# Chunked delta rule and two feed-forward layers: two row products as one run, Silu as the gate, and new positions

## The chip, the cores and the metric

The kernel runs on one core of one Trainium2 chip. The metric is device time in microseconds (us) of one execution, the median of the runs. The engines are TensorE (PE, with its weight loads PEld), VectorE (DVE), ScalarE (ACT), GpSimd (POOL) and SyncE (SP), which here issues the DMA requests. An SPq or PEq in a row is the engine's sequencer.

## What is computed

The inputs are q, k and v (4 batches, 8 heads, 768 positions, 48 features) and beta. Everything is float32.

```python
k_n = k / (norm(k) + 1e-06)
for t in range(S):                      # per batch and head, state is 48 x 48
    y[t] = q[t] @ state
    state = state + beta[t] * outer(k_n[t], v[t] - k_n[t] @ state)
x = y as (3072 tokens, 384)
h = x @ w_in;   x = (h * sigmoid(1.702 * h)) @ w_out      # first layer, 384 -> 2048 -> 384
h = max(x @ w_in2, 0);   out = (h * h) @ w_out2           # second layer, same sizes
```

## The kernel before

**Chunks.** The 768 positions are cut into 12 chunks of 64. Within a chunk the recurrence is a triangular system. For chunk n, `run_a` multiplies keys by keys and queries by keys (for chunk 0 `run_k` and `run_q` do this apart), `solve_in` transposes the result, `solve_norm` finds the key norms, `solve_prep` scales the rows and sets the diagonal of U (L659 to L665), and `solve_loop` inverts the triangles step by step, on POOL for most chunks. For chunks 0 and 1 (`blocks`) it works on 16 x 16 blocks (`solve_blocks`, 15 steps), which `merge` joins with two groups of matmuls. `finish` transposes U to Td (L751). Then come `scale_v` (v times the norms), `run_x` (what the state already holds for these keys), `run_w` (the first 32 rows of the solution), `run_r` (the block that links the two halves, negated back into Td at L858 and L860), `run_v` (the other 32 rows, from Td and both kinds of rows), `run_y` (the chunk's output) and `run_s` (the new state). A float32 matmul of these groups is two TensorE instructions in the trace.

**Tokens.** `run_y` leaves one chunk's 256 tokens in xf_sb; part of them is moved across partitions by six small DMAs, from Td's space (L910). Two chunks make a block of 512 tokens. The first layer takes the blocks in units: `step` is one unit (128 of the 2048 hidden rows): 9 matmuls into a bank h, the gate, and `layer2` adds 9 matmuls into three banks z. Products are exact to float32 by splitting x, the weights and the gated values into a high and a low part (three matmuls for each). The second layer runs behind the first, when no chunk is left. The first 16 units are half as wide (256 columns): 8 for chunk 0's tokens alone, then 8 for chunk 1's.

**The gate of the first layer** (L1029 to L1035): ScalarE writes g = tanh(0.851 h) from h to SBUF; VectorE writes (g + 1) h back into h (L349); ScalarE copies h rounded to ghi; VectorE writes glo = h - ghi. The factor 0.5 is applied when z is taken out.

**Weights** arrive in float32 through three buffers raw, and each is split by ScalarE (a Prelu and two copies), VectorE and VectorE or POOL (`split_w`).

**Order.** All work is put into a list by a planner (`Program`), which knows estimated costs, and sends each operation to its engine's queue in the order in which the planned engines come free; an operation with two possible queues takes the earlier one. Each engine then runs its queue in order. `TUNE` holds numbers for it: `scan`, `gscan`, `solve` and `gsolve` are positions, in units, at which a chunk's groups join the list; `conv` is how many weights are split behind each unit; `holds` makes a group of loads wait for a named result; `gate` adds such a dependence in the plan. `pad` names TensorE entries by their number and puts so many zero matmuls (512 columns, L306) ahead of each; `auto` adds zero matmuls where the plan shows a gap: its first number times the gap, less the second, up to the planned time that is its third. `fills` and `warm` place further zero matmuls, `warm` behind steps of chunk 0's solve (`keep_warm`, L669), where a matmul of one column that reads U comes ahead of them.

The first chain is chunk 0: its keys, its solve on VectorE, merge, w, r, v and `first_y`, which makes x for the first unit without the DMAs.

Of the kernel before, what the change touches and what calls it, by code (L numbers as in the profile page):

```python
# [48 lines left out]
    tiny=(0, 40),  # L49
# [16 lines left out]
class Program:  # L66
# [8 lines left out]
    def __init__(self, queues):  # L75
        self.queues = queues
        self.ops = []
        self.writer, self.readers = {}, {}
        self.free = {q: 0.0 for q in queues}
        self.dma_free = 0.0  # L80
        self.urgent = False
        self.columns = {}
        self.gate, self.idle = (), set()
        self.filler, self.n_pe, self.z_out = None, 0, []
        self.run = self.run_end = self.burst_end = 0.0
# [37 lines left out]
    def flush(self):  # L123
# [22 lines left out]
        while todo:  # L146
# [80 lines left out]
def kernel(  # L227
# [80 lines left out]
    z_open = [0]  # L308
# [341 lines left out]
    def solve_prep(n):  # L650
        s2, U = sm["s2"], U_sb[n % 2]
        gu = gu_sb[n % 2].rearrange("p (i j) -> p i j", i=32)
        K = gu_keys(n)
        if n in TUNE["blocks"]:
# [4 lines left out]
        for e in range(2):  # L659
            R, W = ["dup", "s2", ("U", n % 2)], [("U", n % 2)]  # L660
            o, x, d = U.rearrange("p c i -> p (c i)")[:, e::34], s2[:, e::2], dup_sb[:, e:e + 1]
            if n == 0:
                pg.add("pool", 0.27, lambda en, o=o, x=x, d=d: en.tensor_scalar(out=o, in0=x, scalar1=d, scalar2=None, op0=ALU.mult), R, W)
            else:
                ts(32, R, W, out=o, in0=x, scalar1=d, op0=ALU.mult)  # L665
# [14 lines left out]
    def solve_blocks(n, queue):  # L680

        gu, U = gu_sb[n % 2].rearrange("p (i j) -> p i j", i=32), U_sb[n % 2]
        for j in range(15):
# [27 lines left out]
            pg.add(queue, cost, fn, gu_keys(n) + [("U", n % 2)], [("U", n % 2)] + ((gu_keys(1) if n == 0 else ["tmp1"]) if queue == "dve" else []) + (["first"] if n == 0 and j == 14 else []))  # L711
            if n == 0:
                keep_warm(U[:, 7, j:j + 1], len(pg.ops) - 1, TUNE["warm"][j])
# [96 lines left out]
    def run_w(n):  # L810
        Td = Td_sb[n % 2]
        both, todo = groups(1), []
        for p in range(8):
            for g, ps, A, sl in both:
                for h in range(2):
                    r = 64 * h
                    o = r if g else r + 32
                    todo.append((ps[o:o + 32, p, :], Td[r:r + 32, 8 * g + p, :], w_sb[r:r + 32, 8 * g + p, :], True, True))
        mms((1.05, 1.75), todo, [("Td", n % 2)] + [("Td", n % 2, h) for h in range(2)] + [("W", g, 0, h) for g in range(2) for h in range(2)],
            [A for _, _, A, _ in both], 0.45)  # L820
        return evict_w(n, 0, both)
# [20 lines left out]
    def run_r(n):  # L842

        G, Td = G_sb[n % 2], Td_sb[n % 2]
        ps, A = bank()
        todo = []
        for a in range(NP):
            for h in range(2):
                r = 64 * h
                todo.append((ps[r:r + 32, 32 * a:32 * a + 32], G[r + 32:r + 64, a, 32:64], Td[r + 32:r + 64, a, :], True, True))  # L850
        mms((1.05, 1.75), todo, G_keys(n) + [("Td", n % 2)] + [("Td", n % 2, h) for h in range(2)], [A], 0.2)
        for h in range(2):
            r = 64 * h
            out, in_ = Td[r:r + 32], ps[r:r + 32].rearrange("p (a i) -> p a i", a=NP)

            def fn(e, out=out, in_=in_):
                if e is nc.scalar:
                    e.activation(out=out, in_=in_, func=AF.Copy, scale=-1.0)  # L858
                else:
                    e.tensor_scalar(out=out, in0=in_, scalar1=-1.0, scalar2=None, op0=ALU.mult)  # L860

            pg.add(("act", "dve"), (c_act(512, 32), c_dve(512, False, 32)), fn, [A], [("Td", n % 2, h)])

# [12 lines left out]
    def ws_keys(g):  # L876
        return [("W", g, k, h) for k in range(2) for h in range(2)]

    def run_y(n):
# [17 lines left out]
        for g, ps, A in both:  # L897
# [76 lines left out]
    def layer2(ph, j, f, c0, n, hi, lo, K):  # L974
# [385 lines left out]
```

## Time and profile before

| | us |
|---|---|
| median of 3 runs (lowest, highest) | 976.78 (976.5, 977.99) |
| the profiled execution | 979.03 |
| its span, first to last instruction | 977.2 |
| TensorE busy | 946.9 |
| VectorE busy | 522.7 |
| ScalarE busy | 459.3 |
| POOL busy | 326.1 |

The profile is one execution. An engine's busy time is the time that its instructions cover. The granted clock is the share of full speed (2.4 GHz) that TensorE had in a stretch; 0.50 is 1.2 GHz. In brackets behind an instruction stands how long its engine waited for it and which engine, tile and line released it.

### The profile page before, as it was taken

Reading aid. Unit: us, or ns where it says so; the run is one execution under the profiler, and the core shown is the slowest. Engines: PE = TensorE matmul, PEld = TensorE weight load, DVE = VectorE, ACT = ScalarE, POOL = GpSimd, SP = SyncE. Lnnn points to the kernel's source line nnn. Section 1 sums busy time; section 2 is a strip of 40 time slices with the busy share of each in tenths; the row PEclk is TensorE's granted clock in tenths of the full one; section 3 lists DMA queues with packets and bytes.
Section 4 is the critical chain, followed back from the end, with each engine's and each line's share of the span. In section 5 each row is a group of like instructions: output and inputs, shape, how many; then the busy total and the mean of one; then the engine's idle time right before and its main releaser. Section 6 shows DMA issues by size and latency. Waiting matters only on the chain.

```text
span 977.2 us, 25992 instructions
## 1 busy us (share of the span) xinstructions
PE 946.9 (97%) x11067; PEld 768.5 (79%) x11067; DVE 522.7 (53%) x1038; ACT 459.3 (47%) x934; POOL 326.1 (33%) x702
## 2 busy tenths in 40 slices
PE   7888999999999999999999999999999999999998
PEld 4567877778788878877887888888888888888886
DVE  7767975837566483656536676643433433433332
ACT  4367785444453544445346575642332422422322
POOL 3148885885857658585501000000000000000000
PEclk9679999999999999999999999999999999999999
DMA  5466561413313132221024354220010100000000
GB/s 187 161 196 210 140 203 49 132 29 102 117 65 99 50 110 68 63 79 39 17 78 155 97 159 130 67 65 1 13 52 1 52 14 1 33 0 1 33 1 33
DMA packets 34635, 75.84 MB, mean 78 GB/s; under 512 B 6326, under 2 KB 7382, under 8 KB 34518
## 3 DMA queue, kind: packets, MB, share of 16 engines
q1 hardware_dynamic: 34518, 74.17, 24.4%
q8 instruction: 87, 1.43, 0.6%
q14 instruction: 30, 0.25, 0.1%
HBM read 63.64 MB, written 9.44 MB: 75 GB/s over the span
## 4 chain that ended last, share of the span: by engine, by line
PE 77%; POOL 10%; DVE 6%; issue 3%; ACT 2%; DMA 2%; SPq 0%; POOLq 0%; ACTq 0%; DVEq 0%
PE h L369 35%; PE z L369 34%; PE a L369 7%; POOL tmpp L737 5%; POOL U L741 4%; DMA xf_sb<-Td 1%; DVE glo L342 1%; PE z L306 1%; DVE h L349 1%; DVE Td L751 1%; DVE w_sb L342 1%; ACT w_sb L331 0%; POOL wo_lo L342 0%; POOL p L543 0%; DMA k_sb<-in_kt 0%
## 5 line engine op out<-in xcount | busy, mean ns | idle before, releaser
L326 ACT ACTIVATE g_sb<-h 128x512 f32<-128x512 f32 (+1 forms) x200 | 116.0, 580 | 289.2 <-PE h L369 288.1
L369 PE MATMUL z<-ghi,wo_hi 128*128 128x512 f32 (+1 forms) x600 | 231.5, 386 | 0.0
L369 PE MATMUL z<-glo,wo_hi 128*128 128x512 f32 (+1 forms) x600 | 230.0, 383 | 0.3 <-DVE glo L342 0.3
L369 PE MATMUL z<-ghi,wo_lo 128*128 128x512 f32 (+1 forms) x600 | 229.4, 382 | 0.0
L342 DVE TENSOR_TENSOR glo<-h,ghi 128x512 fp32r<-128x512 f32 (+1 forms) x200 | 133.3, 667 | 83.4 <-ACT ghi L326 81.6
L326 ACT ACTIVATE ghi<-h 128x512 fp32r<-128x512 f32 (+1 forms) x200 | 116.0, 580 | 116.8 <-DVE h L349 58.4
L737 POOL TENSOR_TENSOR tmpp<-U,gu 128x126 f32<-128x126 f32 (+22 forms) x310 | 137.8, 445 | 84.6 <-DVE U L346 61.8
L342 DVE TENSOR_TENSOR h<-g_sb,h 128x512 f32<-128x512 f32 x96 | 66.8, 696 | 173.5 <-ACT g_sb L326 173.5
L741 POOL TENSOR_TENSOR U<-U,tmpp 128x126 f32<-128x126 f32 (+22 forms) x310 | 129.5, 418 | 24.3
L369 PEld LDWEIGHTS z<-ghi,wo_hi 128*128 128x128 f32 x600 | 113.5, 189 | 23.4
L369 PEld LDWEIGHTS z<-glo,wo_hi 128*128 128x128 f32 x600 | 113.5, 189 | 22.9 <-DVE glo L342 0.8
L369 PEld LDWEIGHTS z<-ghi,wo_lo 128*128 128x128 f32 x600 | 113.7, 190 | 22.2
L369 PE MATMUL h<-x_hi,wi_hi 128*128 128x512 f32 (+1 forms) x312 | 125.7, 403 | 4.0 <-DVE glo L342 3.0
L349 DVE SCALAR_TENSOR_TENSOR h<-g_sb,h 128x512 f32<-128x512 f32 (+1 forms) x104 | 67.6, 651 | 115.0 <-ACT g_sb L326 109.7
L369 PE MATMUL h<-x_lo,wi_hi 128*128 128x512 f32 (+1 forms) x312 | 118.3, 379 | 0.0
L369 PE MATMUL h<-x_hi,wi_lo 128*128 128x512 f32 (+1 forms) x312 | 117.7, 377 | 0.0
L369 PE MATMUL h<-x_hi,vi_hi 128*128 128x512 f32 x288 | 112.0, 389 | 0.0
L369 PE MATMUL h<-x_hi,vi_lo 128*128 128x512 f32 x288 | 112.0, 389 | 0.0
L369 PEld LDWEIGHTS h<-x_hi,wi_hi 128*128 128x128 f32 x312 | 59.7, 191 | 20.0 <-DVE glo L342 5.9
L369 PEld LDWEIGHTS h<-x_hi,wi_lo 128*128 128x128 f32 x312 | 59.8, 192 | 10.8
L369 PEld LDWEIGHTS h<-x_lo,wi_hi 128*128 128x128 f32 x312 | 59.9, 192 | 8.2
L369 PEld LDWEIGHTS h<-x_hi,vi_lo 128*128 128x128 f32 x288 | 54.0, 188 | 11.3
(153 smaller groups left out, 1133.4 us busy)
## 6 DMA issues: line engine op xcount, KB each, us to landing
raw<-in_w_in SPq DMA_DIRECT2D x32, 384.0 KB, 3.4
raw<-in_w_out SPq DMA_DIRECT2D x32, 384.0 KB, 3.7
kq<-in_kf SPq DMA_DIRECT2D x44, 256.0 KB, 3.6
kT_sb<-in_kq SPq DMA_DIRECT2D x11, 512.0 KB, 4.7
q<-in_kq SPq DMA_DIRECT2D x11, 512.0 KB, 3.8
k_sb<-in_kt SPq DMA_DIRECT2D x12, 384.0 KB, 3.8
v_sb<-in_vt SPq DMA_DIRECT2D x12, 384.0 KB, 4.7
xf_sb<-zd SPq DMA_DIRECT2D x18, 256.0 KB, 2.8
```

Of the source, the lines that this page charges most:

```text
L306: e.matmul(out=z_ps[KX - 1][:, 0:w], lhsT=z0[:, 0:128], rhs=z0[:, 0:w], start=not z_open[0], stop=not z_open[0])
L326: pg.add("act", c_act(n, kw["out"].shape[0]), lambda e: e.activation(**kw), reads, writes, early)
L342: pg.add(queue, cost, lambda e: e.tensor_tensor(out=out, in0=in0, in1=in1, op=op), reads, writes, early)
L349: pg.add("dve", c_dve(n), lambda e: e.scalar_tensor_tensor(**kw), reads, writes, early)
L369: e.matmul(out=out, lhsT=lhsT, rhs=rhs, start=start, stop=stop)
L737: e.tensor_tensor(out=t, in0=U[:, c0 + lo:c0 + hi, w:w + 1].to_broadcast(shape), in1=gu[:, :w, w:w + 1].rearrange("p i o -> p o i").to_bro ...
L741: e.tensor_tensor(out=y, in0=y, in1=t, op=ALU.add)
L751: pg.add("dve", 0.97, lambda e: e.transpose(out=Td_sb[n % 2].rearrange("p a (c e) -> p c e a", e=2), in_=U_sb[n % 2]), [("U", n % 2)], [(" ...
```

## The change

- `run_r` is gone as a function: its matmuls stand in `run_w`, each behind one of w's, in a bank of their own. Td's link block is copied behind w's rows.
- The gate is Silu(1.702 h) from h to g; ghi and glo are made from g, not from h; z is multiplied by 1/1.702. VectorE's product is gone.
- In chunk 0 the diagonal of U is set ahead of the block product, one half on POOL and one on VectorE, as separate keys; the matmul of `keep_warm` reads another column; `scale_v(0)` can run on VectorE alone.
- The load of a later chunk's queries is planned behind y's six DMAs (`behind_y`); the first queries are loaded and multiplied behind chunk 1's keys (`q_first`), and the loads behind the first keys wait for a later group (`holds`).
- Chunk 1's solve runs on POOL, chunk 2's norms on VectorE; the low parts of the second layer's weights are made on POOL alone; scaling v may go to either engine for chunks 1 to 4.
- Positions, conversions, pads and the planner's fillers have new numbers. Between z's last matmul and its copy no filler is put in.

```diff
-    warm=(0, 1, 0, 2, 0, 1, 1, 0, 1, 0, 1, 0, 0, 0, 1, 0),
-    burst=(2, 7, 120),
-    spread=1.85,
+    warm=(1, 0, 0, 1, 0, 0, 0, 0, 1, 0, 0, 3, 2, 1, 0, 1),
+    burst=(3, 2, 220),
+    spread=1.65,
...
-    slack=0.1,
+    slack=0.2,
-    q_first=1,
+    q_first=0,
-    lead=0,
-    holds=(1, 1, 1),
+    lead=80,
+    holds=(2, 1, 1),
-    conv=(3, 1, 1, 4, 0, 1, 2, 0, 1, 0, 0, 0, 0, 3, 3, 1, 1, 4, 4, 1, 2, 1, 3, 0, 0, 4, 1, 1, 7, 0, 6, 6),
-    lo_both=99,
-    v_pool=2,
+    conv=(4, 1, 0, 5, 1, 3, 1, 3, 0, 0, 0, 1, 0, 3, 0, 0, 1, 3, 4, 2, 2, 4, 1, 1, 1, 4, 1, 1, 4, 0, 3, 7),
+    lo_both=32,
+    v_pool=5,
-    solve1='dve',
-    pad={27: 2, 147: 3, 36: 4, 33: 6, 217: 1, 48: 2, 28: 3, 20: 1, 41: 1, 12: 3},
-    auto=(3.0, 1.3, 290),
-    fills=(2, 0, 0, 0),
-    norm_pool=(1, 2),
+    solve1='pool',
+    pad={217: 1, 12: 1, 41: 3, 90: 1, 11: 1, 263: 4, 35: 6, 229: 4, 50: 1, 150: 3, 154: 3, 29: 2, 226: 3, 27: 2, 259: 2, 284: 1, 31: 5, 306: 3, 309: 1, 44: 4, 143: 2, 273: 4, 180: 3, 264: 2, 34: 1, 32: 3},
+    auto=(6.0, 1.5, 620),
+    fills=(5, 0, 3, 0),
+    norm_pool=(),
-    scan={1: (-4.5, -4.5, -3.0, -2.5, -1.0, 1.0), 2: (11.5, 11.5, 11.5, 11.5, 12.5, 14.5), 3: (14.5, 19.0, 19.5, 19.5, 21.5, 22.0)},
-    gscan=(0.0, 2.0, 2.0, 3.5, 3.5, 7.5),
-    gsolve=(-9.0, -8.0, -2.5, -1.5),
-    solve={2: (-8.0, -7.0, -5.5, -2.5), 3: (3.0, 8.0, 12.0, 12.5), 4: (14.5, 19.0, 21.0, 21.5), 5: (21.5, 24.1, 30.2, 31.5)},
+    scan={1: (-1.5, -1.5, -1.0, 1.0, 1.0, 2.5), 2: (9.5, 9.5, 9.5, 9.5, 9.5, 13.5), 3: (17.0, 20.0, 20.0, 21.0, 21.0, 25.0)},
+    gscan=(1.0, 1.5, 1.5, 3.0, 4.0, 8.0),
+    gsolve=(-11.5, -10.5, -2.5, 0.5),
+    solve={2: (-10.5, -9.5, -7.5, -2.0), 3: (1.5, 6.0, 9.0, 11.5), 4: (11.0, 18.5, 20.5, 22.0), 5: (23.0, 25.1, 29.7, 31.0)},
...
-                if pad:
+                if pad and self.z_open[0] >= 0:
...
+        def diagonal(e):
+            R, W = ["dup", "s2", ("U", n % 2)], [("U", n % 2)] if n else [("U", 0, e)]
+            o, x, d = U.rearrange("p c i -> p (c i)")[:, e::34], s2[:, e::2], dup_sb[:, e:e + 1]
+            if n == 0 and e == 0:
+                pg.add("pool", 0.27, lambda en: en.tensor_scalar(out=o, in0=x, scalar1=d, scalar2=None, op0=ALU.mult), R, W)
+            else:
+                ts(32, R, W, out=o, in0=x, scalar1=d, op0=ALU.mult)
+
+        if n == 0:
+            for e in range(2):
+                diagonal(e)
...
-                keep_warm(U[:, 7, j:j + 1], len(pg.ops) - 1, TUNE["warm"][j])
+                keep_warm(U[:, 7, w - 1:w], len(pg.ops) - 1, TUNE["warm"][j])
...
-           ("dve", "pool") if n < TUNE["v_pool"] else "dve")
+           ("dve", "pool") if 0 < n < TUNE["v_pool"] else "dve")
...
     def run_w(n):
-        Td = Td_sb[n % 2]
+        G, Td = G_sb[n % 2], Td_sb[n % 2]
         both, todo = groups(1), []
+        ps_r, A_r = bank()
...
-                    r = 64 * h
+                    a, r = 8 * g + p, 64 * h
                     o = r if g else r + 32
-                    todo.append((ps[o:o + 32, p, :], Td[r:r + 32, 8 * g + p, :], w_sb[r:r + 32, 8 * g + p, :], True, True))
+                    todo.append((ps[o:o + 32, p, :], Td[r:r + 32, a, :], w_sb[r:r + 32, a, :], True, True))
+                    todo.append((ps_r[r:r + 32, 32 * a:32 * a + 32], G[r + 32:r + 64, a, 32:64], Td[r + 32:r + 64, a, :], True, True))
...
+    def behind_y(load, *args):
+
+        old = pg.gate
+        pg.gate = [y_dma[0]]
+        load(*args)
+        pg.gate = old
...
-                act(TT, [("z", e)], [key], out=zs, in_=z_ps[e], scale=0.5 if ph == 1 else 1.0)
+                act(TT, [("z", e)], [key], out=zs, in_=z_ps[e], scale=1.0 / GATE if ph == 1 else 1.0)
...
         if ph == 1:
-            act(n, [("h", p)], kg, out=g, in_=ps, func=AF.Tanh, scale=GATE / 2)
-            stt(n, [("h", p)] + kg, [("h", p)], out=ps, in0=g, scalar=1.0, in1=ps, op0=ALU.add, op1=ALU.mult)
+            act(n, [("h", p)], kg, out=g, in_=ps, func=AF.Silu, scale=GATE)
+            act(n, kg, khi, out=hi, in_=g)
+            tt(n, kg + khi, klo, lo, g, hi, ALU.subtract)
...
-            put(2, lambda: run_r(m))
...
-                put(4, *[lambda g=g: load_kq(m + 2, g) for g in range(4)], lambda: load_q(m + 2))
+                put(4, *[lambda g=g: load_kq(m + 2, g) for g in range(4)], lambda: behind_y(load_q, m + 2))
```

## Rows read from the trace of the kernel before

**Rows 1.** The page, busy us (share of the span) and instructions.
```profile
PE 946.9 (97%) x11067; PEld 768.5 (79%) x11067; DVE 522.7 (53%) x1038; ACT 459.3 (47%) x934; POOL 326.1 (33%) x702
```
**Rows 2.** Windows by stage; the first line names the columns.
```profile
core 0: us, PE busy (x) PEld busy (x) DVE busy (x) ACT busy (x) POOL busy (x), PEclk, DMA share, GB/s
...
24.80:41.80 17.00, 13.07 (x309) 8.99 (x311) 12.55 (x57) 5.63 (x13) 2.68 (x3) 0.50 0.62 204
...
58.90:69.10 10.20, 8.30 (x214) 7.69 (x215) 5.33 (x13) 8.05 (x19) 2.98 (x10) 0.50 0.44 120
69.10:100.00 30.90, 25.44 (x623) 22.21 (x622) 24.11 (x43) 23.74 (x62) 25.68 (x45) 0.94 0.70 214
100.00:185.00 85.00, 81.52 (x1473) 66.02 (x1474) 63.90 (x133) 58.30 (x133) 66.32 (x131) 0.98 0.46 140
185.00:260.00 75.00, 73.88 (x1273) 58.88 (x1272) 43.52 (x89) 34.29 (x71) 55.81 (x130) 1.00 0.21 62
...
920.00:977.20 57.20, 53.07 (x234) 43.36 (x232) 17.93 (x26) 16.77 (x28) 0.00 (x0) 1.00 0.04 14
```
**Rows 3.** Waits of TensorE: us in total, times, longest.
```profile
PE a L369 <- issue: 6.5, 5, 1.8
...
PE h L369 <- DVE glo L342: 3.0, 7, 0.7
```
**Rows 4.** Timeline of chunk 0's solve: start us, us, what [idle before].
```profile
9.84 1.06 POOL L663 TENSOR_SCALAR U<-sm_s,dup_sb 128x16 f32<-128x16 f32 x2 [2.65 <-issue]
...
10.94 0.68 DVE L697 SCALAR_TENSOR_TENSOR U<-gu,U 128x15 f32<-128x15 f32 x4 [0.56 <-POOL U L663]
...
15.31 0.30 DVE L702 TENSOR_TENSOR U<-U,gu 128x35 f32<-128x35 f32 x2 [0.61 <-PE z L672]
...
16.14 1.55 POOL L342 TENSOR_TENSOR w_sb<-v_sb,nt 128x768 f32<-128x768 f32 x1 [3.74 <-DMA v_sb<-in_vt]
...
16.27 1.57 DVE L702 TENSOR_TENSOR U<-U,gu 128x30 f32<-128x30 f32 x2
```
**Rows 5.** Timeline of TensorE: w of chunk 2, w and r later.
```profile
152.78 0.88 PE L369 MATMUL a<-w_sb,Td 32*32 32x48 f32 x64 [1.43 <-DVE Td L751]
...
358.56 0.39 PE L369 MATMUL z<-glo,wo_hi 128*128 128x512 f32 x1
358.79 0.39 PE L369 MATMUL z<-ghi,wo_lo 128*128 128x512 f32 x1
359.11 0.80 PE L369 MATMUL a<-w_sb,Td 32*32 32x48 f32 x56
...
359.80 1.14 PE L369 MATMUL a<-Td,G 32*32 32x32 f32 x61
...
361.21 0.40 PE L369 MATMUL h<-x_lo,wi_hi 128*128 128x512 f32 x1
```
**Rows 6.** Timelines of TensorE, SP and ScalarE: chunk 1's r, v, y, run_a.
```profile
70.03 1.20 PE L369 MATMUL a<-Td,G 32*32 32x32 f32 x64
...
73.14 0.88 PE L369 MATMUL a<-w_sb,Td 64*32 64x48 f32 x62 [0.45 <-DVE Td L860]
...
79.14 0.33 SPq L313 DMA_DIRECT2D q<-in_kq  x1
...
80.36 3.84 SPq L313 DMA_DIRECT2D xf_sb<-Td  x6
...
86.86 0.42 ACT L326 ACTIVATE x_hi<-xf_sb 128x256 fp32r<-128x256 f32 x1 [2.96 <-DMA xf_sb<-Td]
...
87.88 0.93 PE L369 MATMUL a<-kq 64*32 64x96 f32 x56 [2.95 <-ACT p L331]
```
**Rows 7.** Windows of the fillers (L306) alone: us, PE busy, PEld busy, clock.
```profile
185.00:260.00 75.00, 0.39 (x1) 0.10 (x1) 1.00 0.21 62
```
**Rows 8.** Groups by form: count, busy us, mean ns, idle before.
```profile
L349 DVE SCALAR_TENSOR_TENSOR h<-g_sb,h 128x512 f32<-128x512 f32 x88 | 61.0, 693 | 114.0 <-ACT g_sb L326 108.8 <-ACT xf_sb L326 4.8
...
L346 DVE TENSOR_SCALAR U<-sm_s,dup_sb 128x16 f32<-128x16 f32 x22 | 5.4, 283 | 0.0
...
L326 ACT ACT_TABLE_LOAD x2 | 2.6, 1283 | 0.8 <-PEq L1351 0.8
```

More of the change, by code (lines that the diff above doesn't have):

```diff
@@ L83, in __init__ @@
         self.gate, self.idle = (), set()
-        self.filler, self.n_pe, self.z_out = None, 0, []
+        self.filler, self.n_pe, self.z_out, self.z_open = None, 0, [], [0]
         self.run = self.run_end = self.burst_end = 0.0
@@ L658, in solve_prep @@
             tt(1024, ["s2"] + K, K, gu, gu, s2.rearrange("p (i o) -> p i o", o=1).to_broadcast([128, 32, 32]), ALU.mult)
[L659 to L665, printed above, removed]
+        if n:
+            for e in range(2):
+                diagonal(e)
     def keep_warm(gate, key, parts):
@@ L710, in solve_blocks @@
             cost = 2 * c_pool(2 * m * w) - 0.04 if queue == "pool" else 4 * (0.06 + 0.00104 * m * w) + 0.05
-            pg.add(queue, cost, fn, gu_keys(n) + [("U", n % 2)], [("U", n % 2)] + ((gu_keys(1) if n == 0 else ["tmp1"]) if queue == "dve" else []) + (["first"] if n == 0 and j == 14 else []))
+            pg.add(queue, cost, fn, gu_keys(n) + [("U", n % 2)] + ([("U", 0, e) for e in range(2)] if n == 0 else []), [("U", n % 2)] + ((gu_keys(1) if n == 0 else ["tmp1"]) if queue == "dve" else []) + (["first"] if n == 0 and j == 14 else []))
             if n == 0:
-                keep_warm(U[:, 7, j:j + 1], len(pg.ops) - 1, TUNE["warm"][j])
+                keep_warm(U[:, 7, w - 1:w], len(pg.ops) - 1, TUNE["warm"][j])
     def solve_loop(n, queue, cuts):
@@ L815, in run_w, with fn @@
                 for h in range(2):
-                    r = 64 * h
+                    a, r = 8 * g + p, 64 * h
                     o = r if g else r + 32
-                    todo.append((ps[o:o + 32, p, :], Td[r:r + 32, 8 * g + p, :], w_sb[r:r + 32, 8 * g + p, :], True, True))
-        mms((1.05, 1.75), todo, [("Td", n % 2)] + [("Td", n % 2, h) for h in range(2)] + [("W", g, 0, h) for g in range(2) for h in range(2)],
-            [A for _, _, A, _ in both], 0.45)
-        return evict_w(n, 0, both)
+                    todo.append((ps[o:o + 32, p, :], Td[r:r + 32, a, :], w_sb[r:r + 32, a, :], True, True))
+                    todo.append((ps_r[r:r + 32, 32 * a:32 * a + 32], G[r + 32:r + 64, a, 32:64], Td[r + 32:r + 64, a, :], True, True))
+        mms((1.5, 2.5), todo, G_keys(n) + [("Td", n % 2)] + [("Td", n % 2, h) for h in range(2)] + [("W", g, 0, h) for g in range(2) for h in range(2)],
+            [A for _, _, A, _ in both] + [A_r], 0.45)
+        more = evict_w(n, 0, both)
+        for h in range(2):
+            r = 64 * h
+            out, in_ = Td[r:r + 32], ps_r[r:r + 32].rearrange("p (a i) -> p a i", a=NP)
+            def fn(e, out=out, in_=in_):
+                if e is nc.scalar:
+                    e.activation(out=out, in_=in_, func=AF.Copy, scale=-1.0)
+                else:
+                    e.tensor_scalar(out=out, in0=in_, scalar1=-1.0, scalar2=None, op0=ALU.mult)
+            pg.add(("act", "dve"), (c_act(512, 32), c_dve(512, False, 32)), fn, [A_r], [("Td", n % 2, h)])
+        return more
     def evict_w(n, k, both):
@@ L840, in evict_w @@
         return more
[L842 to L862, printed above, removed]
     def run_v(n):
@@ L1033, in step @@
             tt(n, [("h", p)] + kg, [("h", p)], ps, g, ps, ALU.mult)
-        act(n, [("h", p)], khi, out=hi, in_=ps)
-        tt(n, [("h", p)] + khi, klo, lo, ps, hi, ALU.subtract)
+            act(n, [("h", p)], khi, out=hi, in_=ps)
+            tt(n, [("h", p)] + khi, klo, lo, ps, hi, ALU.subtract)
         prev.append((ph, j, f, c0, n, hi, lo, khi + klo))
@@ L1130 @@
         solve_norm(1)
-        act(32, ["nu"], ["warmed"], out=g_sb[:, 0:32], in_=z32[:, 0:32], func=AF.Tanh)
+        act(32, ["nu"], ["warmed"], out=g_sb[:, 0:32], in_=z32[:, 0:32], func=AF.Silu)
         solve_prep(1)
         more = run_w(0)
-        run_r(0)
         for x in more:
```

11 lines of the change are left out of this document (7 added, 4 removed).

## The prediction, made before the change was run

> **What bounds the kernel now.** I read the page's busy shares first: TensorE is busy 946.9 us of a span of 977.2 us [rows 1], so nearly all of the time is matmuls laid end to end, and a gain must shorten the matmul list, fill TensorE's idle 30 us, or lift its clock. The windows by stage then show where that is possible [rows 2]. From 185 us on TensorE is busy 73.88 of 75 us at full clock, so there only less TensorE work helps; at the end stand 4.1 us (57.2 less 53.07) of output that nothing here touches. The loss is early: in 24.8 to 41.8 and 58.9 to 69.1 the granted clock is 0.50 (the 1.2 GHz level); in 69.1 to 100 TensorE is idle 5.5 us; in 100 to 185 it is idle 3.5 us and the mean clock of 0.98 costs another 1.7 us. The waits of TensorE name the releasers [rows 3]: 6.5 us of "issue" (in stretches of small matmuls) and 3.0 us for glo. The timelines [rows 4 to 6] show who stands behind each.
>
> The sum is made against the profiled span of 977.2 us; that execution took 979.03 us in all, and the median of the runs, 976.78, lies 0.4 us under the span. I take off the same 0.4 us at the end.
>
> **The change part by part.**
>
> *Three waits of the first chain (9.7 to 16.3 us).* (1) Now the two diagonal products on POOL take 9.84 to 10.90 and VectorE's first solve step starts at 10.94 after 0.56 us of waiting [rows 4]. VectorE was free at 10.38; after, one of the two goes to it ahead of the block product and takes 0.28 us (L346, [rows 8]), so the solve starts at 10.66: -0.28 us. (2) The keep-warm matmul reads U's column j, which a later step overwrites; VectorE waited 0.61 us for it [rows 4]. Column w-1 is final after its step, so this wait goes: -0.61. (3) scale_v(0) ran on POOL from 16.14 for 1.55 us, and in that time two VectorE updates of 30 columns took 1.57 us, where a pair of 35 columns took 0.30 at 15.31 [rows 4]: -1.27. On VectorE it comes behind the solve, next to TensorE's first merge; if that cover is gone it costs about 1.0 us. Together **-2.1** (bounds -2.2 to 0). Late next: the queries. Their two loads now go out behind four key loads and behind a later hold, some 2 to 3 us later than at 7 us; their matmuls move behind run_a(1) and have until the solve ends, behind 17 us, so I price that at nothing; uncovered it is those 2 to 3 us, which cancels this term (the upper bound). The 80 one-column matmuls of lead run while TensorE waits for its first keys: nothing.
>
> *Chunk 1's solve from VectorE to POOL.* VectorE loses the solve's 56 small steps, between which the evictions of w and v queued in the first half-clocked stretch. POOL is free in that stretch (2.68 us busy of 17 [rows 2]). **-0.5** (bounds -2 to +1: POOL's operations slow VectorE, as under (3)).
>
> *w and r as one run.* In a full-clock chunk the last large matmul before starts at 358.79, w's 64 small ones at 359.11, r's at about 359.80, and the second large one behind starts at 361.21 [rows 5]. Large ones follow each other every 0.23 us (358.56, 358.79), so w and r cost 361.21 - 358.79 - 2 x 0.23 = 1.96 us. w takes 0.69 us for 64 (10.8 ns each), r from 359.80 to about 360.87, 1.07 us (16.7 each), the rest, 0.2, is changeover. w's go to four places of the array, r's to two, and with fewer places the pace is slower; r's places are others than w's, so in turn each gets more time. Bounds: at r's own pace the whole takes 1.07 + 0.2 (saves 0.7); without any overlap and with a dearer changeover 1.96 + 0.2 (costs 0.2). If 128 go at w's pace, the fastest in the rows, they need 1.38 us and save 0.38. I take -0.45, between that and r's own pace. Ten chunks (2 to 11), of which chunk 2 has its r apart (w alone at 152.78 [rows 5]) and saves one more changeover: **-4.8** (bounds -7.2 to +2).
> The Trainium skill, "TensorE: Matmul & The Clock Gate", section "Back-to-back issue gap", gives about 25 ns as the issue floor of a matmul of 1 to 64 columns; by it 128 would need 3.2 us and no order could gain. The trace does not agree: w's go at 10.8 ns.
>
> *The same in chunks 0 and 1.* Chunk 0: r's result is there with w's and no longer after the copies of w's last rows: **-0.7** (0 to -1.5). Chunk 1: r stands apart at 70.03, and v waits for its copies until 73.14 [rows 6]. In turn with w, which runs as soon as Td is merged, r, v and y can come some us earlier.
>
> *Queries later, y earlier.* The six requests that carry y's rows across partitions go out at 80.36, behind a 512 KB query load of 79.14; ScalarE stands at x_hi for them for 2.96 us, until 86.86, and TensorE at run_a for 2.95 us [rows 6]; then the clock falls, and the mean of 0.94 over 30.9 us costs 1.9 us [rows 2]. Put behind y, the load takes about 2.4 us out of their way (512 KB at the 214 GB/s of [rows 2]). Idle and lost clock are worth 4.8 us; but y itself is put one unit later (18 matmuls of 256 columns, 0.12 us each: 2.2 us). What waits behind the query load on SP's queue are weight loads, 2 us later, with three buffers in hand. **-3.0** (bounds -4.8 to +3).
>
> *Silu.* The product on VectorE falls away: 88 of 0.693 us and 16 shorter ones [rows 8], some 67 us of VectorE, off TensorE's path except where h is held. h is now free after the first activation, not after glo: the 3.0 us of waiting for glo [rows 3] go; in exchange g's single buffer is held until glo is read, which ends in the 4.1 us of a unit. **-2.5** (bounds -3.0 to 0).
>
> *Chunk 2.* w waits 1.43 us for the transposed Td [rows 5], then the clock falls (1.7 us lost). Its solve is asked for earlier and VectorE is lighter: **-1.5** (bounds -3.1 to +1).
>
> *Fillers.* Zero matmuls put ahead of a TensorE entry cost 0.23 us each wherever TensorE would not have waited. The old table's last entries are 147:3 and 217:1; the one filler after 185 us is the latter [rows 7]. From entry 143 on the new table has 36, 25 of them from 217 on, in place of 4: 32 x 0.23 = 7.4 us. The planner's own fillers (auto) come on top wherever it sees a gap over 0.4 us, 0.8 before. Idle there was 3.5 + 1.1 us [rows 2], and half of it is already counted as gone above. I take **+4** (bounds +1 to +7.4). The remaining positions, and the second layer's weights split on POOL alone, lie beside a gapless TensorE, which hides them: nothing; uncovered, a split on POOL is about 0.8 us (half the columns of the 1.55 us of [rows 4]), once for each unit that waits for it.
>
> Sum: -2.1 - 0.5 - 4.8 - 0.7 - 3.0 - 2.5 - 1.5 + 4.0 = -11.1; 977.2 - 11.1 - 0.4 = 965.7, say **966 us**.
>
> **The rivals.**
> *A, no overlap of w and r, or every filler in full.* For it: TensorE takes its list in order. Against: w's own four places already go faster than r's two. Without the 4.8, or with 3.4 more for fillers: 969 to 975, about 971.
> *B, the clock stays up early.* In the two stretches at 0.50 TensorE is busy 13.07 and 8.30 us, fillers included [rows 2]; at full clock at most half of it, 10.7 us, goes. For it: more zeros in the gaps (fills 2 to 8), shorter waits. Against: the issue stalls stay. I counted nothing; with 5 us: about 961, down to 956.
> *C, chunk 1 comes late.* Slower. Chunk 1's y feeds the second half of the first units; each us that its rows land after 86.8 is TensorE idle, then half-clocked, so counts about 1.6 (2.95 us idle brought 1.9 of lost clock). Its solve on POOL, y and s at later places all push it back. It decides from some 8 us later on (11.1 + 2 over 1.6); with 10 us, about 981. Against: POOL is nearly idle from 24.8 to 41.8 us [rows 2].
> *D, the tables.* Slower. A table load takes 1283 ns, and there are two in all [rows 8], though Tanh alternates with the weights' Prelu. If Silu needed another table than Prelu, some 58 loads would come before 185 us: 74 us of ScalarE, which has 34 us free between 69 and 185 [rows 2]: 40 us more than fits, about 1006. The Trainium skill, "ScalarE: Activation LUTs", section "Table sets: the hidden batching unit", says that cheap functions stand in every set; whether Prelu is one of them it does not list, and no row shows it.
> *E, no change:* gains go where TensorE is not waited for, fillers eat the rest: 975 to 978.7.
>
> **How the numbers follow.** Forecast (961 to 970) 0.43, A 0.20, B 0.19, E 0.08, C 0.07, D 0.03. About 0.2% (2 us) is what a measurement here can tell from no change. Faster is the forecast, A and B: 0.82; same 0.08; slower C and D, 0.10. The range leaves out C, D, most of E's upper half and B's last part: 956 to 976.
>
> **What would show it.** First solve step near 10.7 and no VectorE pair of 1.57 us; all behind it some 3 us earlier at chunk 0's end; w and r of a chunk together near 1.5 us; no wait of TensorE for glo; y's six requests ahead of the query load; less idle than 5.5 us before 100 us; and behind 185 us the fillers, and whether idle stands in front of them. The prediction is wrong if w and r keep 1.96 us, if the fillers stand in a gapless stretch, or if chunk 1's rows land after 90 us.

## The result, and the profile after

The changed kernel takes **989.09 us** (median; 988.31 to 989.36), the kernel before, beside it on the same chip, 976.71: a ratio of 1.0123 (95% interval 1.0105 to 1.014), 12 us slower. The prediction, 966 and faster, was wrong. The profiled execution took 988.31 us, its span is 986.6 (before 977.2). (The profiled executions of e4, e7 and e12 took far longer than the other runs of the same kernels, 1052 to 2418 us, so for those three only the other times are used.)

The windows of the changed kernel that answer to [rows 2], and one more:
```profile
24.80:41.80 17.00, 12.65 (x390) 8.44 (x394) 9.39 (x24) 10.28 (x24) 10.40 (x25) 0.63 0.76 264
58.90:69.10 10.20, 8.34 (x233) 6.99 (x234) 5.65 (x19) 2.48 (x5) 2.15 (x2) 0.83 0.25 83
69.10:100.00 30.90, 26.93 (x664) 22.63 (x650) 24.49 (x40) 24.49 (x61) 25.55 (x44) 1.00 0.63 201
100.00:185.00 85.00, 78.16 (x1464) 63.21 (x1470) 58.77 (x113) 57.90 (x130) 66.98 (x130) 1.00 0.45 141
185.00:260.00 75.00, 72.10 (x1261) 55.60 (x1264) 35.76 (x76) 32.33 (x69) 58.81 (x125) 0.98 0.20 62
260.00:520.00 260.00, 254.89 (x4081) 204.49 (x4081) 116.91 (x228) 118.20 (x234) 164.89 (x356) 0.99 0.21 67
```
The last of these windows in the kernel before:
```profile
260.00:520.00 260.00, 259.05 (x4097) 208.63 (x4096) 146.51 (x286) 120.43 (x246) 150.05 (x348) 1.00 0.23 73
```
Up to 100 us the change as a whole gained: the clock is higher in all three windows, and TensorE is idle 4.0 us (30.90 less 26.93) from 69.1 to 100, where it was 5.5 [rows 2]. Behind 100 us, and most of all behind 185 us, where the prediction saw a gapless TensorE, the gain is lost. There TensorE is idle 6.8, 2.9 and 5.1 us, together 14.85; before it was 5.55 (3.5, 1.1 and, from 260 to 520, 0.95). A count of the matmuls into h and z shows where the time goes. At 185 us the changed kernel has started 177 of those with 512 columns, the kernel before 174; at 320 us 579 and 620, and at 520 us 1272 and 1315. So nearly all of the loss arises between 185 and 320 us: 41 matmuls, at 0.23 us each 9.4 us, as much as the two profiled spans differ. VectorE is lighter (468.8 us busy in all, before 522.7), POOL heavier (375.9 for 326.1). TensorE's waits from 100 to 320 us say for whom (us in total, times, longest):
```profile
PE a L369 <- DVE Td L759: 8.2, 3, 4.5
PE z L369 <- DVE glo L342: 2.6, 2, 1.6
PE a L369 <- DVE sm_nu L566: 1.4, 1, 1.4
PE a L369 <- DVE w_sb L342: 1.0, 1, 1.0
```
The line for Td in the kernel before, same stretch:
```profile
PE a L369 <- DVE Td L751: 1.9, 2, 1.4
```
8.2 us go to three waits for Td, the solved system that comes from POOL's solve (chunks 2, 4 and 6: 1.09, 2.60 and 4.53 us). TensorE's timeline at the longest of them, and POOL's in the same stretch:
```profile
286.49 0.39 PE L369 MATMUL z<-ghi,wo_lo 128*128 128x512 f32 x1
291.41 0.28 PE L369 MATMUL a<-w_sb,Td 32*32 32x48 f32 x1 [4.53 <-DVE Td L759]
```
```profile
271.01 0.25 POOL L749 TENSOR_TENSOR U<-U,tmpp 128x31 f32<-128x31 f32 x1
271.34 1.55 POOL L745 TENSOR_TENSOR tmpp<-U,gu 128x110 f32<-128x110 f32 x1
272.97 0.41 POOL L749 TENSOR_TENSOR U<-U,tmpp 128x110 f32<-128x110 f32 x1
273.46 0.58 POOL L745 TENSOR_TENSOR tmpp<-U,gu 128x30 f32<-128x30 f32 x1
...
288.75 0.43 POOL L745 TENSOR_TENSOR tmpp<-U,gu 128x110 f32<-128x110 f32 x1
289.27 0.40 POOL L749 TENSOR_TENSOR U<-U,tmpp 128x110 f32<-128x110 f32 x1
289.74 0.22 POOL L745 TENSOR_TENSOR tmpp<-U,gu 128x16 f32<-128x16 f32 x1
290.04 0.23 POOL L749 TENSOR_TENSOR U<-U,tmpp 128x16 f32<-128x16 f32 x1
```
From 270.7 us on, chunk 7's first steps (31, 30, 58 columns) stand in turn with chunk 6's last (110, 108, 96), and chunk 6's solve, which TensorE waits for, ends at 290.3 only. Chunk 7's steps take about 10 us of that stretch, more than the 4.53 us waited. The granted clock falls to the 1.2 GHz level from 208.0 to 211.4 and from 289.9 to 296.75 us, at two of the waits for Td; the kernel before has one such stretch behind 100 us, of 3.4 us (154.4 to 157.8), and then none before the output. TensorE works in 8.7 us of the two stretches (in the second it waits until 291.41), so half clock costs some 4.4 us. Waits for Td and half clock are thus 12.6 us, for 1.9 and 1.7 before: 9.0 us more, close to what the spans differ. (The expectations below reckon with 5.1 us of half clock, which counts the waiting in.)

Other rows that answer to those of before. The w and r of chunk 7 as one run, without a gap (TensorE, to set beside [rows 5]):
```profile
326.63 0.39 PE L369 MATMUL h<-x_hi,wi_lo 128*128 128x512 f32 x1
326.95 0.23 PE L369 MATMUL a<-w_sb,Td 32*32 32x48 f32 x1
326.96 0.21 PE L369 MATMUL a<-Td,G 32*32 32x32 f32 x1
...
328.57 0.39 PE L369 MATMUL h<-x_lo,wi_hi 128*128 128x512 f32 x1
```
By the prediction's reckoning from [rows 5], 328.57 - 326.63 - 2 x 0.23 = 1.48 us for 1.96: 0.48 saved. The chain of chunk 0 (VectorE), and chunk 1's row requests (SP):
```profile
8.69 1.90 DVE L352 STREAM_TRANSPOSE gu<-G 128x1024 f32<-128x1024 f32 x1
11.44 0.67 DVE L705 SCALAR_TENSOR_TENSOR U<-gu,U 128x15 f32<-128x15 f32 x4
16.07 0.32 DVE L710 TENSOR_TENSOR U<-U,gu 128x30 f32<-128x30 f32 x2
18.13 1.05 DVE L759 STREAM_TRANSPOSE Td<-U 128x512 f32<-128x512 f32 x1
```
```profile
80.11 4.55 SPq L313 DMA_DIRECT2D xf_sb<-Td  x6
87.50 0.42 SPq L313 DMA_DIRECT2D q<-in_kq  x1
```
The 1.57 us pair and the 0.61 us wait of [rows 4] are gone; the first step came at 11.44 and not near 10.7. The six requests for y's rows stand ahead of the query load; run_a(0) of the next chunk starts at 85.48, for 87.88 [rows 6].

### The profile page after: what moved, and what is told of

It reads as the page before. It is cut to its first block, busy times and chain, and to the rows that moved or that the text cites. A ratio compares the mean times of both kernels' runs of the same rounds, so it can differ in the third digit from the quotient of the medians.

```text
span 986.6 us, 26198 instructions
## 1 busy us (share of the span) xinstructions
PE 950.6 (96%) x11202; PEld 768.6 (78%) x11223; DVE 468.8 (48%) x873; ACT 461.2 (47%) x926; POOL 375.9 (38%) x738
## 4 chain that ended last, share of the span: by engine, by line
PE 68%; POOL 15%; DVE 8%; issue 4%; ACT 2%; DMA 2%; SPq 1%; DVEq 0%; POOLq 0%; ACTq 0%
PE h L369 31%; PE z L369 31%; POOL tmpp L745 8%; POOL U L749 7%; PE a L369 5%; PE z L306 1%; DVE glo L342 1%; DMA kq<-in_kf 1%; DVE gu L342 1%; DVE c L349 1%; DVE x_lo L342 1%; DMA q<-in_kq 1%; POOL p L543 0%; DVE Td L759 0%; DVE gu L360 0%
## 5 line engine op out<-in xcount | busy, mean ns | idle before, releaser
L745 POOL TENSOR_TENSOR tmpp<-U,gu 128x126 f32<-128x126 f32 (+22 forms) x310 | 149.2, 481 | 60.0 <-DVE U L346 37.2
L342 DVE TENSOR_TENSOR glo<-g_sb,ghi 128x512 fp32r<-128x512 f32 (+1 forms) x104 | 74.7, 719 | 161.2 <-ACT ghi L326 157.7
L749 POOL TENSOR_TENSOR U<-U,tmpp 128x126 f32<-128x126 f32 (+22 forms) x310 | 132.5, 427 | 24.3
L342 DVE TENSOR_TENSOR glo<-h,ghi 128x512 fp32r<-128x512 f32 x96 | 66.4, 692 | 55.7 <-ACT ghi L326 55.5
L326 ACT ACTIVATE ghi<-h 128x512 fp32r<-128x512 f32 x96 | 57.2, 596 | 57.7 <-DVE h L342 57.0
L331 ACT ACTIVATE w_sb<-a 32x384 f32<-32x384 f32 x92 | 44.3, 482 | 43.9 <-PE a L369 40.4
```

Of the source, the lines that this page charges most:

```text
L326: pg.add("act", c_act(n, kw["out"].shape[0]), lambda e: e.activation(**kw), reads, writes, early)
L331: e.activation(out=out, in_=in_, func=AF.Copy)
L342: pg.add(queue, cost, lambda e: e.tensor_tensor(out=out, in0=in0, in1=in1, op=op), reads, writes, early)
L745: e.tensor_tensor(out=t, in0=U[:, c0 + lo:c0 + hi, w:w + 1].to_broadcast(shape), in1=gu[:, :w, w:w + 1].rearrange("p i o -> p o i").to_bro ...
L749: e.tensor_tensor(out=y, in0=y, in1=t, op=ALU.add)
```

## The experiments

Ratios are to the kernel before on the same chip, each with its 95% interval; 0.1% is about 1 us. First a table, of single profiled executions: chunk 2's Td (start of the transpose), TensorE's idle time from 100 to 520 us, and fillers (L306, weight loads counted, as some matmul records are missing) in the same stretch.

| kernel | ratio | Td of chunk 2 | idle, us | fillers |
|---|---|---|---|---|
| before | 1 | 113.61 | 5.6 | 4 |
| changed | 1.0123 (1.0105 to 1.014) | 121.26 | 14.9 | 36 |
| e1_serial | 1.0046 (1.0033 to 1.0058) | 118.83 | 8.5 | 36 |
| e2_nofill | 1.0113 (1.0087 to 1.0139) | 122.79 | 18.9 | 0 |
| e3_serial_nofill | 1.0059 (1.0034 to 1.0085) | 119.15 | 15.1 | 0 |
| e5_before_serial | 0.9997 (0.9982 to 1.0012) | 113.62 | 5.0 | 4 |
| e9_before_serial_silu2 | 1.0097 (1.0070 to 1.0123) | 120.99 | 11.7 | 4 |
| e13_short_solve | 0.9938 (0.9922 to 0.9953) | 117.99 | 0.9 | 36 |
| e16_same_order_all | 0.9916 (0.9902 to 0.9930) | 112.43 | 4.0 | 4 |
| e17_before_short | 0.9942 (0.9925 to 0.9958) | 110.94 | 3.0 | 4 |
| e18_short_nofill | 0.9867 (0.9842 to 0.9891) | 119.50 | 3.5 | 0 |

**e1 to e4: interleaving, fillers, shapes.** The edit of e1 gives the planner one dependence more:
```diff
-            pg.add(queue, cost, fn, gu_keys(n) + [("U", n % 2)], [("U", n % 2)])
+            pg.add(queue, cost, fn, gu_keys(n) + [("U", n % 2)], [("U", n % 2)], after=solved[0] if j == 0 else ())
+        if queue == "pool":
+            solved[0] = (len(pg.ops) - 1,)
```


> The changed kernel with one dependence more in the planner: on POOL a solve begins only behind the last step of the solve before it, so that the steps of two chunks no longer stand in turn. Nothing else is edited; a place the planner chooses anew may move a filler. Theory T (the new positions interleave two solves on POOL, Td comes late, TensorE waits 8.2 us for it and then runs 10.2 us at half clock, 5.1 us lost): the waits for Td near 158, 207 and 291 us go and with them the half clock, 989 less 8 to 13, about 978 (974 to 981). Rival F (the 34 late zero matmuls at 0.23 us, 7.8 us, are the loss): stays within 2 us of 989. Rival S (the new shape of the instructions itself costs: w and r in turn, Silu): stays above 984 too.

982.74 us: 6.4 us back by the medians, 7.5 by the ratios, less than Theory T said. Between 69 us and the output no half-clocked stretch is left, and the waits for Td from 100 to 320 us fell from 8.2 to 1.8:
```profile
PE a L369 <- DVE Td L763: 1.8, 2, 1.5
```
So the interleaving is one cause. How much of these 6 to 8 us is its own stays open, as the dependence also made the planner move over a tenth of VectorE's operations to other places. The 4.5 us that remain over before have another cause.

e2 and e3 cut `pad` at entry 143 and set `auto=(6.0, 1.5, 100)`:

> The changed kernel without the fillers planned from entry 143 on, by table and by the planner (about 26 to 34 zero matmuls of 0.23 us, 6 to 7.8 us); the solves stay interleaved on POOL. Rival F: all of it comes back, about 981 to 983. Theory T: the waits for Td stay, those fillers that stood in front of a waiting entry turn into waiting, so that only some 3 to 5 us come back: 984 to 987, and the half-clocked stretches behind 200 us remain.

> Both edits: solves one behind the other on POOL, and no filler from entry 143 on. If both theories hold and their prices add (8 to 13 us of late Td, 6 to 7 us of fillers): 969 to 974, below the kernel before. If the fillers were cover for waits that only the interleaving makes: about as the first plus the fillers' full 6 to 7 us. If S holds (the shape of the instructions costs): above 980.

990.06 and 985.16 us: neither is faster, though some 8 us of fillers are gone (36 at 0.23 us) and every other operation keeps its place. The idle time grew by 4.0 and 6.6 us (table), and the waits for Td from 100 to 320 us grew to 11.6 and 5.1. In e2 the mean clock from 100 to 185 us fell from 1.00 to 0.96 as well, 3.4 us. So the fillers stood in front of waits: rival F falls, and so does "both add".

e4 puts the new shapes (w and r in turn, Silu, the three waits out) into the kernel before, with its own numbers for positions and e1's edit:

> The kernel before, with its own positions, queries, fillers and engines, but with w and r in turn as one run, Silu in place of Tanh, scaling and product, the three waits of the first chain out, and solves one behind the other on POOL (so that the planner does not interleave them for the new costs). Theory T with the prices of the prediction (w and r 4.8 to 5.5, Silu 2.5, three waits 2.1): about 967 (963 to 971). Rival S: no gain or a loss, 975 or above, and the span of w and r of a full-clock chunk stays at 1.96 us.

994.35 us (ratio 1.0143, 1.0107 to 1.0178). That Theory T blames the *new* positions alone falls here: the old numbers are worse with the new shapes.

**e5 to e8: one shape at a time at the old positions; lead.**

> The kernel before with the one dependence added: a solve on POOL begins only behind the last step of the solve before it. It is the control for the runs on the old positions: before has one place only where five steps of two solves stand in turn (chunks 2 and 3). Expected within 2 us of the kernel before. If it is 10 us or more slower, the dependence itself spoils the old positions, and the 16 us that the run with old positions and all new shapes lost are not the shapes' doing.

977.11 us, no difference: a control.

> As the control, and w and r in turn as one run; nothing else of the change. If the matmuls saved are worth what the windows of the changed kernel show (a period of 42.2 us for 42.6, chunks 3 to 10), 4 to 5 us below the control. If TensorE's supply and not its list sets the time before 320 us, the saving comes back as waiting, and only chunks 8 to 11 gain: 1 to 2 us. Slower than the control by 5 us or more: the one run is what cost the 16 us of the run with all new shapes.

979.72 (1.0015, 0.9998 to 1.0032). Each run of w and r without a gap takes 1.60 us from the last large matmul ahead to the first behind, for 2.08 before, yet the whole gained nothing: Td of chunk 2 came at 122.88.

> As the control, and Silu in place of Tanh and the product; nothing else of the change. The prediction's term: 2.5 us below the control (the waits for glo ahead of first-layer matmuls go). Rival: the waits for glo only move to the second-layer matmuls, 0 to +2 us. Slower than the control by 5 us or more: Silu is what cost the 16 us of the run with all new shapes.

990.17 (1.0118, 1.0089 to 1.0147); see e9.

> The changed kernel with solves one behind the other on POOL (first run of this study) and lead 0 in place of 80: without the 80 one-column matmuls that hold TensorE to 6.6 us, while the keys were there at 4.7 us in the kernel before. If they are what made the first solve start at 11.4 instead of 10.7 us, the solve starts 0.8 to 1.1 us earlier and so does all of chunk 0: about 981.5 (0.8 to 1.3 us less than the first run). Rival: the clock is lower in the head without them, no gain or 1 us lost.

982.39 (1.0038, 1.0025 to 1.0051). The first solve step starts at 10.66 us, 0.78 earlier than in the changed kernel, as the prediction had it without the 80 matmuls; the time is 0.8 us less than e1's by the ratios, within the uncertainty.

**e9 to e12: Silu, w and r, POOL, each undone or relieved.** e9 is e7 with the change's rule for fillers (`if pad and self.z_open[0] >= 0`):

> The control (the kernel before with solves one behind the other on POOL) with Silu in place of Tanh and the product, and the changed kernel's rule that no zero matmul is put between the end of a z group and its eviction; for a profile of the old positions with Silu. The run without that rule took 990 us, 13 above the control (there a zero matmul cleared a z bank ahead of its eviction, so a part of the output was lost; the work was all done). If Silu with the old positions is what costs: again 988 to 992, and the profile names the wait: if it is the single buffer of g, ScalarE stands for glo and TensorE behind it for evictions; if it is the plan, the waits are for Td or s of late chunks. If the missing rule did it: 975 to 978.

988.17 (1.0097). The rule is not the cause, then; Silu with the order that the planner writes for it is. TensorE waits 5.8 us for Td from 60 to 260 us, 1.4 in e5, so 4.4 of the 11 us lost are seen as later solves. POOL in e9 shows one way: a weight split stands in its queue for ScalarE while solve steps wait behind it.
```profile
108.85 0.69 POOL L743 TENSOR_TENSOR U<-U,tmpp 128x96 f32<-128x96 f32 x1
111.97 1.21 POOL L342 TENSOR_TENSOR wi_lo<-c,wi_hi 128x384 fp32r<-128x384 f32 x1 [2.43 <-ACT wi_hi L326]
113.14 0.58 POOL L739 TENSOR_TENSOR tmpp<-U,gu 128x91 f32<-128x91 f32 x1
```
e10 and e11 undo Silu and the one run in e1's kernel:

> The changed kernel with solves one behind the other and Silu undone (Tanh and VectorE's product again, new positions and all else kept). If Silu itself costs time: 970 to 979, below the first run's 982.7. If Silu is worth the 2.5 us of the prediction: about 985. If the plan is tuned to it as the old plan was to Tanh: 988 or more, with more waiting and fillers between 100 and 320 us, and the same 13 us in the other direction.

> The changed kernel with solves one behind the other and w and r apart again (two lists, r at its own place of the new positions). Each run in turn is 0.48 us shorter in a gapless stretch (2.08 to 1.60), so the prediction's term says about 5 us more than the first run's 982.7: 987. Rival (TensorE waits for its supply up to 320 us, so what the list saves there turns into waiting): only the gapless chunks 7 to 11 count, +2 to +2.5: about 985.

984.43 (1.0064, 1.0038 to 1.0089) and 986.25 (1.0081, 1.0054 to 1.0108). With the new numbers for positions each part seems to be worth something: Silu 1.8 us, which these intervals don't tell from nothing, and the one run 3.5, between both expectations.

> The changed kernel with solves one behind the other, and POOL relieved: chunk 1's solve on VectorE again and scale_v on POOL for chunk 1 only, as in the kernel before. If POOL (busy 72.7 of 85 us from 100 to 185) is what makes Td of chunks 1 to 3 late (53.7, 118.8, 159.9 us for 47.0, 113.6, 151.7), Td comes back to about 47 and 114 and the idle and filler time of TensorE from 100 to 320 us falls from 13.6 to about 6 us: 976 to 979. Rival (Td's lateness there costs nothing, the supply of TensorE is set by the places of the chain's steps): 981 to 985.

990.34 (1.0111, 1.0080 to 1.0141): slower, but with a new order on every engine, so it decides nothing about POOL.

The trouble with e4, e6, e7, e9 and e12, and in part with e1, e8, e10 and e11, is this: whatever changes a planned cost or a dependence makes the planner write another order for all engines, and the run measures that order. The last six keep the order of the kernel that they start from and change durations alone (e18 also leaves out fillers).

**e13 and e17: shorter solves in either kernel, same order.** POOL's steps work on a third of their columns, while the planner reckons with all:
```diff
+                if queue == "pool":
+                    parts = [(lo, lo + max(1, (hi - lo) // 3), t[:, 0:max(1, (hi - lo) // 3)]) for lo, hi, t in parts]
```


> The changed kernel as it is, every engine's order unchanged, but POOL's solve steps of chunks 2 to 11 work on a third of their columns (the solves are left incomplete, the output is not the reference's; POOL's time alone is meant). Theory U (Td late from POOL is the loss between 100 and 320 us): the waits for Td (8.2 us) and the half clock behind them (5.1 us) go: 989 less 12 to 15, about 975 (973 to 978), though the 11.5 us of fillers behind 44 us are still there. Rival P (the places of the other steps are worse): 984 or above, with the idle time between 100 and 320 us now in front of other matmuls.

> The kernel before, every engine's order unchanged, with POOL's solve steps of chunks 2 to 11 on a third of their columns (the solves are left incomplete, the output is not the reference's). If the change is what made Td late: little to gain here, the 1.4 us wait of chunk 2's successor and its half clock, and part of the 4.2 us of idle time between 185 and 520: 2 to 5 us below before, 972 to 975. If before loses as much to POOL as the changed kernel does: 15 us or more below, about 960.

972.12 and 972.55 us. By the ratios the changed kernel gains 18.1 us (1.0123 to 0.9938), the kernel before 5.7 (1 to 0.9942). All waits of TensorE in e13 from 100 to 320 us that the view lists:
```profile
PE a L369 <- DVE Td L761: 0.3, 1, 0.3
PE h L369 <- DVE x_lo L342: 0.2, 1, 0.2
```
Theory U holds: the changed kernel loses 18.1 - 5.7 = 12.4 us more to POOL's solves than before does, within the intervals the whole 12 us. With shorter solves the two kernels are even. What the edit takes away is the time of POOL's steps with all that hangs on it: beside the waits for Td, those for glo (2.6), sm_nu (1.4) and w_sb (1.0) are gone too.

**e18: e13 without the late fillers.**

> The changed kernel with the shortened solves of the earlier run (972.1; output likewise not the reference's) and without the fillers planned from entry 143 on (36 of 0.23 us). With nothing left to wait for, each filler stands in a gapless stretch and its removal brings 6 to 8 us: 964 to 967, which is the prediction's number and its filler term (4, up to 7.4). If the fillers still stand in front of waits: 970 to 972.

965.13 us (ratio 0.9867, 0.9842 to 0.9891): 7.0 less than e13. The fillers that cost nothing in e2 cost nearly their full price (8 us) once nothing waits. That the time is near the predicted 966 is chance in part: here before's own 5.7 us for POOL are out too. Against e17 the change without its late fillers gains 7.4 us; the prediction's sum without the filler term was 15.1.

**e14: a later solve in the kernel before, same order.** Ten memsets of POOL's scratch ahead of chunk 2's first step:

> The kernel before, every engine's order unchanged, with ten memsets of POOL's scratch ahead of the first step of chunk 2's solve (some 3 to 5 us; the trace gives it). Theory U: Td of chunk 2 comes that much later than 113.6, TensorE waits at w of chunk 2 and, since POOL is late for chunk 3 too, again there, and the clock falls: 3 to 8 us slower, 980 to 985. Rival P (there is slack): within 1 us of before.

```profile
72.50 2.63 POOL L732 MEMSET tmpp<- 128x136 f32 x10
```
980.16 us (1.0019, 1.0003 to 1.0035), 1.9 us for 2.6 us of POOL: below the 3 to 8 of Theory U, above rival P's 1. Td came at 117.12, idle time rose to 7.3. But the trace doesn't show the way that Theory U gave. w of chunk 2 starts without a wait, as before; waits for Td are 2.1 us from 100 to 320 us, before 1.9. TensorE's longest wait in that stretch comes earlier and is for glo, behind VectorE operations that ran slowly beside POOL's selects (1.41 us for a split that took 0.55 at 99.07 us in the kernel before):
```profile
100.76 1.41 DVE L342 TENSOR_TENSOR wo_lo<-c,wo_hi 128x384 fp32r<-128x384 f32 x1
100.62 1.15 POOL L543 TENSOR_SCALAR_AFFINE_SELECT p<-p 64x1024 f32<-64x1024 f32 x1
102.56 0.44 PE L369 MATMUL h<-x_hi,wi_hi 128*128 128x256 f32 x1 [2.38 <-DVE glo L342]
```
So e14 doesn't show how much slack chunk 2's Td has.

**e15 and e16: the parts in the old order.** Silu is written over h in PSUM, and the planner still reckons with the product; then both lists at r's place, from chunk 4 on:
```diff
-            act(n, [("h", p)], kg, out=g, in_=ps, func=AF.Tanh, scale=GATE / 2)
-            stt(n, [("h", p)] + kg, [("h", p)], out=ps, in0=g, scalar=1.0, in1=ps, op0=ALU.add, op1=ALU.mult)
+            act(n, [("h", p)], kg, out=ps, in_=ps, func=AF.Silu, scale=GATE)
+            pg.add("dve", c_dve(n), lambda e: None, [("h", p)] + kg, [("h", p)])
...
+            pg.ops[-1][2] = lambda e: pend.append((todo, both[0][2]))
...
+                first, bank_w = pend.pop()
+                for x in first + todo if bank_w == A else [x for two in zip(first, todo) for x in two]:
```


> The control (before with solves one behind the other, 977.1) with Silu written over h in its PSUM bank, no VectorE product, and the order of every engine exactly the control's (the planner still reckons with the product). The prediction's 2.5 us for waits on glo that go, with the rest as before: 974 to 976. Rival (Silu itself costs, as in the run that lost 11 us): 985 or above.

> As the run with Silu and the control's order, and w and r in turn for chunks 4 to 11 (both put at r's place, which follows w's directly; eight times 0.48 us), and the keep-warm matmul that reads the finished column. Durations alone change, no place. If each part is worth what its row shows when nothing moves: 3.8 for w and r, 1 to 2.5 for Silu, up to 0.6 for the column: 970 to 973, faster than both kernels. If what the list saves turns into waiting for the chain: 975 to 977.

973.93 us (0.9961, 0.9946 to 0.9975) and **970.08** (0.9916, 0.9902 to 0.9930), faster than both kernels by 8.2 and 20 us. Silu is worth 3.5 us against the control, the one run with the column 4.4 more, for 8 x 0.48 + 0.6 = 4.4 from rows. The windows of e16 show TensorE gapless again from 185 us on:
```profile
100.00:185.00 85.00, 81.60 (x1466) 67.16 (x1466) 56.84 (x118) 58.12 (x132) 68.09 (x134) 0.96 0.47 141
185.00:260.00 75.00, 75.00 (x1342) 60.11 (x1341) 35.24 (x71) 34.17 (x72) 61.01 (x141) 1.00 0.22 68
260.00:520.00 260.00, 259.45 (x4067) 208.67 (x4058) 115.69 (x240) 124.25 (x254) 143.78 (x334) 1.00 0.24 74
```

## Why the prediction was wrong, point by point

**The step that failed** is "The remaining positions [...] lie beside a gapless TensorE, which hides them: nothing", and with it the reading behind it, that from 185 us on "only less TensorE work helps". A busy share of 73.88 of 75 us does not say how much slack the engines have that supply the busy one: the kernel before itself gains 5.7 us from shorter solves (e17). POOL, busy 66 of 85 us in [rows 2], was never asked when it is done. The change loses 12.4 us more to POOL's solves (e13 against e17), 6 to 8 of them by interleaving (e1, which moved other operations too).

**Chunk 2 (-1.5)** failed with it, and the row was misread: the w at 152.78 in [rows 5] is chunk 3's (Td of chunks 0 to 3 starts at 19.60, 47.01, 113.61 and 151.66 us), and so is the r that stands apart. Chunk 2's Td came at 121.26, not earlier; chunk 3's w came at 158.89, again behind 1.43 us of waiting (put down to sm_nu), and w of chunks 4 and 6 waited 2.60 and 4.53 us.

**Chunk 1's solve on POOL (-0.5, to +1).** Td of chunk 1 came at 52.99 us for 47.01; what that cost in time no run separates (e12 was to).

**w and r (-4.8)** were right in size: 0.48 each for 0.45 in a stretch without a gap, and with the order kept 4.4 us together with the column (e16). What the one run is worth in the changed kernel, where TensorE waits, is open: e11 says 3.5 us, but with another order. By these rows 128 go in 1.48 us, 11.6 ns each. The issue floor of about 25 ns that the Trainium skill states ("TensorE: Matmul & The Clock Gate", section "Back-to-back issue gap") is not seen here either.

**Chunk 0's r with w (-0.7)** brought nothing: from the start of w to that of v it took 7.44 us (29.38 to 36.82), before 7.46 (26.71 to 34.17).

**Silu (-2.5).** The waits of matmuls into h for glo went, but 4.3 us of waits of matmuls into z for glo came in their place. In the old order and in PSUM Silu is worth 3.5 us. What the prediction missed is an operand: glo = g - ghi now reads two tensors from SBUF, where h came from PSUM, and POOL's solve steps beside it are slower. POOL's groups from 185 to 520 us (multiply and add of a step; mean ns is the second number behind the bar), of the changed kernel, of e10 (e1 with Tanh) and of e15 (before's order, Silu in PSUM):
```profile
L745 POOL TENSOR_TENSOR tmpp<-U,gu 128x126 f32<-128x126 f32 (+22 forms) x230 | 110.3, 480 | 45.9 <-DVE U L346 28.6
L749 POOL TENSOR_TENSOR U<-U,tmpp 128x126 f32<-128x126 f32 (+22 forms) x230 | 94.6, 411 | 18.0
```
```profile
L747 POOL TENSOR_TENSOR tmpp<-U,gu 128x126 f32<-128x126 f32 (+22 forms) x227 | 96.4, 425 | 51.4 <-DVE U L346 34.2
L751 POOL TENSOR_TENSOR U<-U,tmpp 128x126 f32<-128x126 f32 (+22 forms) x227 | 87.8, 387 | 17.8
```
```profile
L739 POOL TENSOR_TENSOR tmpp<-U,gu 128x126 f32<-128x126 f32 (+22 forms) x227 | 99.1, 437 | 63.2 <-DVE U L346 46.0
L743 POOL TENSOR_TENSOR U<-U,tmpp 128x126 f32<-128x126 f32 (+22 forms) x227 | 88.4, 389 | 17.8
```
A step takes 891 ns in the changed kernel (480 + 411; e1 896, e9 906, e11 891), all with g in SBUF, and 812 in e10, 826 in e15 and e16, 823 before: 65 to 95 ns more on each of 31 steps, by estimate 2 to 3 us later Td for each chunk. The Trainium skill, "GPSIMD Engine Reference", section "1. Specifications", says that POOL shares its SBUF interfaces with VectorE and that there is contention with VectorE instructions of two SBUF inputs. These rows agree. No two runs differ in the operand alone, so how much of the time of e9 or the changed kernel is made of this is not shown.

**Three waits (-2.1).** Two went as reckoned (0.61 and 1.27). "The 80 one-column matmuls of lead [...]: nothing" failed: they end at 6.7 us while the keys were multiplied from 4.74 before, so the solve starts at 11.44 for 10.66 (e8). And what was left of the gain, Td at 18.13 for 19.60, was lost ahead of w (29.38 for 26.71): an "issue" stall of 2.68 us stands there in the merge's small matmuls (the kernel before has one of 1.71); what causes it no row shows.

**Queries, y earlier (-3.0)** held as a mechanism: run_a starts 2.4 us earlier and the window's clock is 1.00; no run gives its price. **Fillers (+4)** depend on the rest: nothing in e2, where TensorE waits, 7.0 in e18, where it does not. **Tables (rival D)**: two table loads, as before. No rival named this loss. Rival C has its sign, but chunk 1's rows came early.

Open: how the some 5 us of late solves beside the interleaving divide between POOL's slower steps, its other work (chunk 1's solve, scale_v) and the places of the solves.

## What to carry to other kernels

A gapless engine is not one with slack behind it: before pricing a moved step at nothing, follow the engine that supplies the busy one and see when each delivery ends and when it is needed. Where a planner writes the order, a new cost is a new order; measure a part with the old order pinned, and only then decide on positions (pinned, w and r in turn and Silu over h in PSUM gave 8 us; replanned, with g in SBUF and the other edits, the kernel lost 12). When an operand moves from PSUM to SBUF, look at which other engines work in SBUF at that time.

## What the runs showed of the hardware, not expected

POOL's solve steps are some 8 to 12% slower in the kernels in which VectorE's glo subtraction has both inputs in SBUF (891 to 906 ns for 812 to 826 a step). The multiply of 110 columns at 271.34 us in the changed kernel took 1.55 us, where one of the same size took 0.43 at 288.75; VectorE updated the state and scaled v by nt (768 columns from SBUF, from 271.63 for 0.95) in that time. In e14 it went the other way: VectorE's split of 384 columns took 1.41 us beside POOL's select, 0.55 without it.
